# Attention, a rational MoE and a second MoE on one core: one scale chain for both halves of a weight chunk, five places for its float32 forms, and bounds spread by products with ones

## The chip, the cores and the metric

The kernel runs on one core of one Trainium2 chip. The metric is device time in microseconds (us), lower is better. Time before: 1236.59 us, the median of three runs (1235.79 to 1240.24).

## What is computed

```python
def _attn_ref(q, k, v, tau):                       # 4 batches, 8 heads, 576 rows, 64 wide
    scores = scale * np.matmul(q, k.transpose(0, 1, 3, 2))
    thresh = np.max(scores, axis=-1, keepdims=True) - tau
    scores = np.where(scores >= thresh, scores, -1000000000.0)
    ...
    return np.matmul(attn, v).astype(np.float32)

def _moe_ref(x, w_in, w_out, a, b):                # 2304 tokens, 512 -> 2048 -> 512
    h = x @ w_in
    ...
    g = P / (Q + 1e-06)                            # P cubic in h, Q quadratic in |h|
    return (g @ w_out).astype(np.float32)

def _moe2_ref(x, w_in, w_out):
    h = x @ w_in
    g = np.where(pos, h, np.where(neg, 0.0, (h + beta) ** 2 / (4.0 * beta)))
    return (g @ w_out).astype(np.float32)
```

The attention's output is the first expert's input, and the first expert's output the second's. The weights come as 64-bit floats.

## The kernel before

**Order of work.** For each of four batches b the first expert (m = 0) and then the second (m = 1) run over three token blocks j of 192 tokens and eight chunks i of 256 hidden columns: 192 steps in all, 24 to a phase. A step is `first_product` (24 matmuls of 192 columns, line L863, tile `ph`), a nonlinearity on ACT and DVE (`rational`, lines L744 to L757, for the first expert, `quadratic`, L808 to L810, for the second), a split of its result into two float16 parts (L209 on ACT, L213 on POOL, tile `gg`), and, three steps later, `second_product` (24 matmuls, L877, tile `acc`). The attention of batch 0 runs ahead of all steps in a transposed form (`first_attention`: `row_max` with DVE maxima L544, `transposed`, `sums`, `divide`). The attention of batches 1 to 3 runs beside the steps as 36 softmax rows of 128 queries each (`att_rows`: maximum L442, exponential L403, threshold L404, splits L412 to L415, a transposing DMA L417, products L430). A priority, `at(...)`, says where on the line of steps each piece belongs, and a scheduler writes the order of each engine's queue by these priorities and its own clock. Each engine runs its queue in that order.

**Weights.** Each chunk of an expert has two halves, x = 0 (`w_in`) and x = 1 (`w_out`), 16 halves per expert. A half is loaded (tile `rw`, 1 MB, L242), and three DVE instructions on 128x1024 words turn the 64-bit words into float32 (`as_float`, L229 to L231, tile `wt`). These float32 forms turn through N_WT = 3 places. Then comes the half's scale chain in `convert`:

- PE multiplies the bfloat16 tops by themselves (8 matmuls, L254, tile `pg`), and DVE takes the largest of each row (L255).
- `everywhere` spreads that bound over all partitions: a product of the bound, broadcast as the stationary operand, with the identity (L188, 128 columns of float32, two instructions) and a DVE maximum over the 128 columns (L189, tile `mw`).
- `root` makes a power of two and its inverse from it: three DVE instructions of one column, L169, L172 and L173 (tiles `f_w` and `pw`).
- `split` scales the float32 form in place on ACT (L218), copies it to float16 (L209) and lets POOL subtract in four pieces (L213). Only then is the place free.

The first expert's halves go into the resident chunks `wc` while `first_attention` runs, 16 halves over 45 steps of it (`make_half`), and a copy of each chunk goes to a scratch in memory. The second expert's halves (`stage_half`, tiles `wh`, two places of the same size as a `wt` place) follow and go to the scratch alone. `prep_pair` spreads the two bounds of q and k of a head pair in the same way (L188 twice, tile `pmmqke`; L189 on 256 columns, tile `mqke`), 16 times in the run.

Of the kernel before, what the change touches and what calls it, by code (L numbers as in the profile page):

```python
# [10 lines left out]
F32 = mybir.dt.float32  # L11
I32 = mybir.dt.int32
# [31 lines left out]
def tile_attention_moe_moe2(  # L44
# [148 lines left out]

    wide = w1_in.dtype != F32
# [7 lines left out]
    f_w = [[small(NCH, f"f_w{m}{x}", True) for x in range(2)] for m in range(2)]  # L202
    f_max = [[None, None], [None, None]]
    gram = small(NCH, "gram", True)
# [16 lines left out]
    def as_float(raw, name):  # L221
# [6 lines left out]
        t = mp.tile([P, E], I32, name="wt" + name, tag="wt", bufs=N_WT)  # L228
# [5 lines left out]
    def convert(m, i, x, dst, on_vector):  # L234

        if x == 0:
            raw = rp.tile([P, KT, CF * words], raw_type, name=f"rw{m}_{i}_0", tag="rw")
            src = w_in_dram[m][:, i * CF * words : (i + 1) * CF * words].rearrange("(kt p) f -> p kt f", p=P)
        else:
            raw = rp.tile([P, NF, DM * words], raw_type, name=f"rw{m}_{i}_1", tag="rw")  # L240
            src = w_out_dram[m][i * CF : (i + 1) * CF, :].rearrange("(f p) d -> p f d", p=P)
        (A if m == 0 and i == 0 else Q).dma_start(raw, src)  # L242
        name = f"{m}_{i}_{x}"
        src = as_float(raw.rearrange("p a b -> p (a b)"), name)
        hi, lo = dst[:, 0:E], dst[:, E : 2 * E]
        columns = m == 0 and x == 0
        bound = gram[:, i : i + 1] if columns else small(1, "mb" + name)
        pg = ps_1.tile([P, 512], F32, name="pg" + name, tag="aux")
        parts = NF if columns else 1
# [5 lines left out]
        V.tensor_reduce(bound, pg[:, 0 : parts * P], axis=AX.X, op=ALU.max)  # L255
        s = root("pw" + name, f_w[m][x][:, i : i + 1], everywhere("mw" + name, bound, 1), 2.0**64, even=m == 1 and x == 1)
        split(hi, lo, src, s, on_vector)
        if i == NCH - 1 and (m, x) != (0, 0):
            f_max[m][x] = small(1, f"f_max{m}{x}", True)
            V.tensor_reduce(f_max[m][x], f_w[m][x], axis=AX.X, op=ALU.max)  # L260
# [73 lines left out]
    def prep_pair(b, pr, on_vector=True):  # L334
# [12 lines left out]
        s = root(f"qkr{b}_{pr}", f, everywhere(f"mqke{b}_{pr}", mx, 2), 2.0**96, n=2)  # L347
# [342 lines left out]
    def moe1_consts(b):  # L690
# [6 lines left out]
        if b == 0:  # L697
# [3 lines left out]
            V.tensor_reduce(norm, gram, axis=AX.X, op=ALU.max)  # L701
# [187 lines left out]
    for n in range(N_FIRST):  # L889
        with at(36 * n / N_FIRST - 40):  # L890
            next(att)
        while halves and len(halves) * N_FIRST > 2 * NCH * (N_FIRST - 1 - n):
            with at(2.4 * (2 * NCH - len(halves)) - 39.5):
                i, x = halves.pop(0)
                make_half(0, i, x, chunks[0, i], False)
# [82 lines left out]
```

## Time and profile before

| | |
|---|---|
| median of three runs | 1236.59 us |
| profiled execution, its own time | 1239.17 us |
| its span, first to last instruction | 1237.1 us |
| busy in that span: PE, DVE, ACT, POOL | 1095.3, 979.3, 839.5, 542.7 us |
| mean granted clock of TensorE | 0.963 |

The profiled execution is 2.6 us above the median, and 2.1 us of its time lie outside the span. A busy share over the whole span mixes stretches with different limits. The rows further down are therefore taken by stretch: up to 230 us the first attention and the weights, then the 192 steps, the first 48 of them beside the attention of batch 1.

### The profile page before, as it was taken

To read this page: it belongs to the slowest core of one execution; us is meant where nothing else is said; L and a number is where in the kernel's file an instruction comes from. 1 tells how busy PE (TensorE), PEld (TensorE's weight loads), DVE (VectorE), ACT (ScalarE), POOL (GpSimd) and SP (SyncE) were. 2 spreads that over 40 slices of the span, in tenths; PEclk is the share of its full clock that TensorE was granted. 3 is DMA by queue.
4 is the path that set the end of the run, shared out by engine and by line. 5 is a ranking of instruction groups with operands and counts; after the bars stand their busy time and mean duration, and the time that the engine had idled before them with its cause. 6 is when DMAs were issued, how large, how long until landed. Compare 5 with 4: busy or idle time off the path is not lost.

```text
span 1237.1 us, 31750 instructions
## 1 busy us (share of the span) xinstructions
PE 1095.3 (89%) x12636; PEld 988.4 (80%) x12636; DVE 979.3 (79%) x2362; ACT 839.5 (68%) x1532; POOL 542.7 (44%) x698
## 2 busy tenths in 40 slices
PE   2778788588899999898888998998899999999998
PEld 1445456477888989898778888997888998999997
DVE  8887896999997377799997766899996768896431
ACT  2577777698887377677875766887675667775332
POOL 2445545656666266322564454223563553222221
PEclk9888888899899999999999999999999999999999
DMA  7677576635269158813785639422984467007000
GB/s 220 224 205 252 210 266 238 220 93 137 49 151 249 29 111 185 218 28 90 183 225 95 115 64 250 136 50 68 242 195 71 81 171 221 15 2 261 15 14 27
DMA packets 217845, 175.51 MB, mean 142 GB/s; under 512 B 179680, under 2 KB 190944, under 8 KB 209504
## 3 DMA queue, kind: packets, MB, share of 16 engines
q1 hardware_dynamic: 216464, 171.38, 52.6%
q8 instruction: 99, 1.62, 0.5%
q10 hardware_dynamic: 1232, 2.10, 0.5%
q14 instruction: 50, 0.41, 0.1%
HBM read 106.83 MB, written 21.50 MB: 104 GB/s over the span
## 4 chain that ended last, share of the span: by engine, by line
PE 40%; DVE 24%; DMA 11%; POOL 9%; issue 9%; ACT 6%; SPq 1%; DVEq 0%; ACTq 0%; POOLq 0%
PE acc L877 15%; PE ph L863 15%; DMA eT<-hl 8%; POOL hl L415 3%; PE pv L613 2%; PE pv L430 2%; DVE t L746 2%; POOL wh L213 2%; DVE e L404 2%; DVE t L751 2%; DVE sc L442 2%; POOL gg L213 1%; DVE t L757 1%; DVE t L748 1%; DVE t L747 1%
## 5 line engine op out<-in xcount | busy, mean ns | idle before, releaser
L877 PE MATMUL acc<-gg,wc 128*128 128x192 f16 x4608 | 427.6, 247 | 10.9 <-DVE mye L189 4.9
L863 PEld LDWEIGHTS <-wc 128*128 128x128 f16 x4608 | 388.9, 99 | 24.4 <-issue 16.5
L877 PEld LDWEIGHTS <-wc 128*128 128x128 f16 x4608 | 384.1, 98 | 12.6 <-issue 11.2
L213 POOL TENSOR_TENSOR gg<-t,gg 128x384 f16<-128x384 f32 x192 | 192.9, 1006 | 380.1 <-ACT gg L209 308.0
L863 PE MATMUL ph<-xT,wc 128*128 128x192 f16 x2304 | 218.1, 252 | 13.3 <-DVE t L748 13.2
L863 PE MATMUL ph<-yT,wc 128*128 128x192 f16 x2304 | 213.4, 246 | 3.7 <-DVE t L748 2.5
L415 POOL TENSOR_TENSOR hl<-e,hl 128x256 f16<-128x256 f32 x216 | 160.6, 764 | 0.0
L209 ACT CAST gg<-t 128x384 f16<-128x384 f32 x192 | 96.9, 508 | 75.1 <-DVE t L810 36.8
L809 DVE SCALAR_TENSOR_TENSOR t<-t,c 128x384 f32<-128x384 f32 x96 | 66.2, 690 | 88.9 <-ACT t L808 87.0
L404 DVE SCALAR_TENSOR_TENSOR e<-sc,nt,e 128x576 f32<-128x576 f32 x108 | 97.5, 903 | 28.1 <-ACT e L403 27.9
L413 POOL TENSOR_TENSOR hl<-e,hl 128x64 f16<-128x64 f32 x108 | 42.3, 391 | 147.7 <-ACT hl L412 134.0
L403 ACT ACTIVATE e<-sc,nt,con 128x576 f32<-128x576 f32 x108 | 93.3, 864 | 4.6 <-POOL hl L415 0.2
L808 ACT ACTIVATE t<-ph,c 128x384 f32<-128x384 f32 x96 | 63.9, 667 | 45.6 <-PE ph L863 45.3
L430 PE MATMUL pv<-v,eT 128*128 128x65 f16 (+3 forms) x1680 | 71.4, 195 | 25.2 <-DMA eT<-hl 24.1
L442 DVE TENSOR_SCALAR_CACHE_REDUCE sc<-s 128x576 f32<-128x576 f32 x108 | 80.8, 748 | 15.2 <-PE s L397 14.5
L412 ACT CAST hl<-e 128x576 f16<-128x576 f32 x108 | 72.1, 667 | 28.6 <-DVE e L404 28.0
L430 PEld LDWEIGHTS <-eT 128*128 128x128 f16 (+1 forms) x1680 | 64.0, 101 | 33.9 <-DMA eT<-hl 30.0
L744 ACT ACTIVATE t<-ph,sc 128x384 f32<-128x384 f32 x96 | 55.3, 576 | 50.6 <-PE ph L863 50.4
L213 POOL TENSOR_TENSOR wc<-wt,wc 128x256 f16<-128x256 f32 x64 | 55.1, 894 | 63.8 <-ACT wc L209 63.8
L749 ACT ACTIVATE t<-t,lc 128x384 f32<-128x384 f32 x96 | 67.8, 708 | 15.3 <-DVE t L746 14.9
L213 POOL TENSOR_TENSOR wh<-wt,wh 128x256 f16<-128x256 f32 x64 | 58.9, 950 | 35.8 <-ACT wh L209 35.7
L751 DVE SCALAR_TENSOR_TENSOR t<-t,ka,t 128x384 f32<-128x384 f32 x96 | 67.7, 705 | 8.7 <-ACT t L750 8.3
(238 smaller groups left out, 1910.9 us busy)
## 6 DMA issues: line engine op xcount, KB each, us to landing
wc<-scratch SPq DMA_DIRECT2D x56, 1024.0 KB, 5.9
rw<-in_moe_w_in_dram SPq DMA_DIRECT2D x15, 1024.0 KB, 5.7
rw<-in_moe_w_out_dram SPq DMA_DIRECT2D x15, 1024.0 KB, 5.4
scratch<-wc SPq DMA_DIRECT2D x8, 1024.0 KB, 4.5
scratch<-wh SPq DMA_DIRECT2D x16, 512.0 KB, 3.7
rqk<-in_q_dram SPq DMA_DIRECT2D x16, 256.0 KB, 3.1
rqk<-in_k_dram SPq DMA_DIRECT2D x16, 256.0 KB, 3.1
kT<-qkT SPq DMA_DIRECT2D x26, 144.0 KB, 2.5
```

Of the source, the lines that this page charges most:

```text
L209: A.copy(hi, src)
L213: G.tensor_tensor(lo[:, p], src[:, p], hi[:, p], op=ALU.subtract)
L403: A.activation(e, s, AF.Exp, bias=nb, scale=con[:, 0:1])
L404: V.scalar_tensor_tensor(e, s, th, e, op0=ALU.is_ge, op1=ALU.mult)
L412: A.copy(hi, e)
L415: G.tensor_tensor(lo_w[:, p], e[:, whole][:, p], hi[:, whole][:, p], op=ALU.subtract)
L430: T.matmul(pv[rows, 0:w], eT[:, c, cols], vv[:, h * NT + x if x < NT else H * NT + h, at : at + w], start=(n == 0), stop=(n == len(blocks) ...
L442: V.tensor_scalar(s, banks[:, 0:S], 1.0, -LARGEST, op0=ALU.mult, op1=ALU.max, accum_out=mx)
L749: A.activation(r, u, AF.Ln, bias=lc[:, 1:2], scale=lc[:, 0:1])
L751: V.scalar_tensor_tensor(s, s, ka[:, 0:1], r, op0=ALU.add, op1=ALU.mult)
L863: last = T.matmul(ph[:, f, :], w[:, wx, kt, f * P : (f + 1) * P], rhs, start=(n == 0), stop=(n == 3 * KT - 1))
L877: T.matmul(dst, w[:, wx, f, d * P : (d + 1) * P], gg[:, gx, f, :], start=(i == 0 and f == 0 and n == 0 and d % 2 == 0), stop=(i == NCH - 1 ...
```

## The change

- `make_half` handles the first expert's two halves of a chunk together. At x = 0 it loads, turns to float32 and takes the maxima (one per 128 columns, so two, into `gram`). At x = 1 it does the same with one maximum, then three products of one column with a constant tile of ones (L301, L302 of the changed file, six instructions where float32 takes two each) put the two bounds into two columns of PSUM, one `root` of two columns reads them there, and both halves are split. The column sums over the partitions take the place of the maxima, so no L189 follows.
- The float32 forms of the first expert turn through five places: the three of `wt` and the two of `wh`, which the second expert uses later.
- `total`, the product with ones, takes the place of `everywhere` in `prep_pair` and for the second expert's x = 1 halves.
- `gram` is 24 columns wide instead of 8, and its largest value is taken over the two columns that belong to `w_in`.

```diff
+    def total(name, src, n):
+
+        pm = ps_1.tile([P, 512], F32, name="ps" + name, tag="aux")[:, 0:n]
+        T.matmul(pm, one.to_broadcast([P, P]), src, start=True, stop=True)
+        return pm
...
-    def as_float(raw, name):
+    turn = [0]
+
+    def as_float(raw, name, first):
...
-        t = mp.tile([P, E], I32, name="wt" + name, tag="wt", bufs=N_WT)
+        n = turn[0] % (N_WT + N_WH)
+        turn[0] += 1
+        if first and n >= N_WT:
+            t = mp.tile([P, E], I32, name="wt" + name, tag="wh", bufs=N_WH)
+        else:
+            t = mp.tile([P, E], I32, name="wt" + name, tag="wt", bufs=N_WT)
...
-        s = root("pw" + name, f_w[m][x][:, i : i + 1], everywhere("mw" + name, bound, 1), 2.0**64, even=m == 1 and x == 1)
+        spread = (everywhere if x == 0 else total)("mw" + name, bound, 1)
+        s = root("pw" + name, f_w[m][x][:, i : i + 1], spread, 2.0**64, even=x == 1)
...
-    def make_half(m, i, x, wc, on_vector):
-        convert(m, i, x, wc[:, x * HALF : (x + 1) * HALF], on_vector)
-        if x == 1:
-            with at(8 + i):
-                Q.dma_start(scratch[m][i], wc)
+    first = {}
+
+    def make_half(i, x, wc):
+        first[x] = load_raw(0, i, x)
+        pg = ps_1.tile([P, 512], F32, name=f"pg0_{i}_{x}", tag="aux")
+        parts = 1 if x else NF
+        squares(pg, first[x], parts)
+        bound = gram[:, i]
+        V.tensor_reduce(bound[:, NF:] if x else bound[:, 0:NF], pg[:, 0 : parts * P].rearrange("p (n q) -> p n q", q=P),
+                        axis=AX.X, op=ALU.max)
+        if x == 0:
+            return
+        pm = ps_1.tile([P, 512], F32, name=f"psw0_{i}", tag="aux")[:, 0:2]
+        for c in range(NF):
+            T.matmul(pm[:, 0:1], one.to_broadcast([P, P]), bound[:, c : c + 1], start=c == 0, stop=c == NF - 1)
+        T.matmul(pm[:, 1:2], one.to_broadcast([P, P]), bound[:, NF:], start=True, stop=True)
+        s = root(f"pw0_{i}", f_w1[:, i], pm, 2.0**64, n=2)
+        for n in range(2):
+            split(wc[:, n * HALF : n * HALF + E], wc[:, n * HALF + E : (n + 1) * HALF], first[n], s[:, n : n + 1], False)
...
-        s = root(f"qkr{b}_{pr}", f, everywhere(f"mqke{b}_{pr}", mx, 2), 2.0**96, n=2)
+        s = root(f"qkr{b}_{pr}", f, total(f"mqke{b}_{pr}", mx, 2), 2.0**96, n=2)
```

The change also moves instructions, since the scheduler writes all queues anew. Line numbers of the changed kernel are higher: L169 and L172 keep their numbers, L188 stays, L229 to L231 become L246 to L248, L254 becomes L267, L255 becomes L280 and L295, L209 becomes L219, L218 becomes L228, L442 becomes L485, L544 becomes L587, L601 becomes L644, L746 to L757 become L789 to L800.

DVE's queue around the third chunk of the first expert, before. `wt_2_1` is the float32 form of chunk 2, half 1; `pw_2_0_s` and `pw_2_1_s` end the chains of its halves; `mx_1` are row maxima of the attention.

```order
L229 TENSOR_SCALAR wt_2_1_628<-rw_2_1_626 128x1024
L230 SCALAR_TENSOR_TENSOR wt_2_1_628<-rw_2_1_626,wt_2_1_628 128x1024
L544 TENSOR_REDUCE mx_1_554<-sm_00_555 128x1
L231 SCALAR_TENSOR_TENSOR wt_2_1_628<-rw_2_1_626,wt_2_1_628 128x1024
L255 TENSOR_REDUCE gram<-pg_2_0_513 128x1
L544 TENSOR_REDUCE mx_1_554<-sm_01_559 128x1
L189 TENSOR_REDUCE mw_2_0_523<-pmmw_2_0_524 128x1
L169 TENSOR_SCALAR f_w_135<-mw_2_0_523 128x1
L172 TENSOR_SCALAR f_w_135<-f_w_135 128x1
L173 RECIPROCAL pw_2_0_s<-f_w_135 128x1
L229 TENSOR_SCALAR wt_3_0_758<-rw_3_0_756 128x1024
L544 TENSOR_REDUCE mx_1_554<-sm_02_618 128x1
```

DVE's queue at the same place of the program, now. The chain of the whole chunk 2 ends with `pw_2_s`.

```order
L587 TENSOR_REDUCE mx_1_517<-sm_12_661 128x1
L172 TENSOR_SCALAR f_w_137<-f_w_137 128x2
L295 TENSOR_REDUCE gram<-pg_3_0_727 128x2
L173 RECIPROCAL pw_2_s<-f_w_137 128x2
L587 TENSOR_REDUCE mx_1_517<-sm_13_665 128x1
L587 TENSOR_REDUCE mx_1_517<-sm_t 128x4 x2
L587 TENSOR_REDUCE mx_1_517<-sm_r 128x1
L587 TENSOR_REDUCE mx_1_517<-sm_rt 128x1
L613 TENSOR_TENSOR mx_1_517<-mx_1_517 128x9
L616 TENSOR_SCALAR pcs_759<-mx_1_517 128x9
L618 SCALAR_TENSOR_TENSOR mx_1_517<-pcs_759,mx_1_517 128x9
L246 TENSOR_SCALAR wt_4_1_1086<-rw_4_1_1084 128x1024
```

Before, the chain of half 0 ends right behind the conversion of half 1, and the conversion of `wt_3_0` follows. Now the conversions of `wt_3_0`, `wt_3_1` and `wt_4_0` stand ahead of the chunk's one chain, and `wt_4_1`, which takes the place of `wt_2_0`, comes nine rows behind it.

ACT's queue for chunk 2, before: `low`, `et` belong to the attention.

```order
L218 ACTIVATE wt_2_0_509<-wt_2_0_509,pw_2_0_s 128x1024
L601 ACTIVATE low_0_4_718<-st_0_4_704,con_0_175 128x576
L209 CAST wc_2_148<-wt_2_0_509 128x1024
L601 ACTIVATE low_1_0_794<-st_1_0_786,con_0_175 128x576
L604 ACTIVATE et_0_4_717<-st_0_4_704,con_0_175 128x576
L604 ACTIVATE et_1_0_793<-st_1_0_786,con_0_175 128x576
```

ACT's queue for chunk 2, now: `x` and `d` are copies of the attention's sums.

```order
L228 ACTIVATE wt_2_0_486<-wt_2_0_486,pw_2_s 128x1024
L228 ACTIVATE wt_2_1_588<-wt_2_1_588,pw_2_s 128x1024
L664 COPY x_0_500<-pv_0_0_515 64x288
L663 COPY d_0_501<-pv_0_0_516 64x288
L664 COPY x_0_500<-pv_0_0_516 64x288
L644 ACTIVATE low_1_1_825<-st_1_1_817,con_0_173 128x576
L219 CAST wc_2_149<-wt_2_0_486 128x1024
L644 ACTIVATE low_1_2_842<-st_1_2_834,con_0_173 128x576
L219 CAST wc_2_149<-wt_2_1_588 128x1024
```

Half 0's copy to float16, on which POOL's subtraction waits, stood two rows behind its scaling; now the scaling of half 1 and four rows of the attention stand between.

DVE's queue in the first phase of steps, batch 0, from step 17 on (`t_0_2_1` is block 2, chunk 1 of the first expert), before. `sc`, `nt`, `e`, `xs`, `xT` belong to the attention rows of batch 1.

```order
L747 TENSOR_TENSOR t_0_2_1_3482<-t_0_2_1_3482,ph_0_2_1_3456 128x384
L444 TENSOR_SCALAR nt_1_0_0_5045<-mx_1_0_0_5044,con_1_3965 128x1
L465 TENSOR_TENSOR xs_0_2_4497<-pv_0_2_4444,rd_0_2_4494 128x128
L751 SCALAR_TENSOR_TENSOR t_0_2_0_3384<-t_0_2_0_3384,ka_1935,t_0_2_0_3383 128x384
L748 SCALAR_TENSOR_TENSOR t_0_2_1_3482<-t_0_2_1_3482,ka_1935,ph_0_2_1_3456 128x384
L476 TENSOR_TENSOR xT_1_3942<-xt_0_1_4417,xT_1_3942 128x64
L404 SCALAR_TENSOR_TENSOR e_0_2_2_4877<-sc_0_2_2_4873,nt_0_2_2_4872,e_0_2_2_4877 128x576
L757 SCALAR_TENSOR_TENSOR t_0_2_0_3383<-t_0_2_0_3383,t_0_2_0_3384 128x384
L442 TENSOR_SCALAR sc_1_0_1_5082,mx_1_0_1_5080<-s_1_0_1_5075 128x576
L746 SCALAR_TENSOR_TENSOR t_0_2_2_3581<-t_0_2_2_3581,qc 128x384
L747 TENSOR_TENSOR t_0_2_2_3582<-t_0_2_2_3582,ph_0_2_2_3556 128x384
L444 TENSOR_SCALAR nt_1_0_1_5081<-mx_1_0_1_5080,con_1_3965 128x1
```

DVE's queue from the same step on, now.

```order
L790 TENSOR_TENSOR t_0_2_1_3385<-t_0_2_1_3385,ph_0_2_1_3359 128x384
L800 SCALAR_TENSOR_TENSOR t_0_2_0_3288<-t_0_2_0_3288,t_0_2_0_3289 128x384
L791 SCALAR_TENSOR_TENSOR t_0_2_1_3385<-t_0_2_1_3385,ka_1852,ph_0_2_1_3359 128x384
L447 SCALAR_TENSOR_TENSOR e_0_2_1_4721<-sc_0_2_1_4717,nt_0_2_1_4716,e_0_2_1_4721 128x576
L794 SCALAR_TENSOR_TENSOR t_0_2_1_3385<-t_0_2_1_3385,ka_1852,t_0_2_1_3384 128x384
L789 SCALAR_TENSOR_TENSOR t_0_2_2_3484<-t_0_2_2_3484,qc 128x384
L800 SCALAR_TENSOR_TENSOR t_0_2_1_3384<-t_0_2_1_3384,t_0_2_1_3385 128x384
L790 TENSOR_TENSOR t_0_2_2_3485<-t_0_2_2_3485,ph_0_2_2_3459 128x384
L791 SCALAR_TENSOR_TENSOR t_0_2_2_3485<-t_0_2_2_3485,ka_1852,ph_0_2_2_3459 128x384
L794 SCALAR_TENSOR_TENSOR t_0_2_2_3485<-t_0_2_2_3485,ka_1852,t_0_2_2_3484 128x384
L789 SCALAR_TENSOR_TENSOR t_0_2_3_3631<-t_0_2_3_3631,qc 128x384
L790 TENSOR_TENSOR t_0_2_3_3632<-t_0_2_3_3632,ph_0_2_3_3606 128x384
```

Rows of the attention stood between the steps before; now the steps stand closer together. By the lists of the two queues 16 maxima L442 of batch 1 stand ahead of the first `quadratic` (step 24) before, and 9 now; ahead of step 29 they are 17 and 9, ahead of step 47 34 and 35, and from step 64 on the two lists differ by two rows at most.

## Rows read from the trace of the kernel before

**Rows 1.** Stretches: length, busy us (instructions) of PE, PEld, DVE, ACT, POOL; clock, DMA

```profile
0.00:45.00 45.00, 18.99 (x121) 11.52 (x121) 39.30 (x102) 15.55 (x25) 10.31 (x25) 1.00 0.63 197
45.00:230.00 185.00, 147.49 (x897) 95.75 (x898) 150.75 (x321) 136.77 (x214) 98.64 (x110) 0.84 0.71 238
230.00:370.00 140.00, 116.37 (x1321) 107.34 (x1319) 136.11 (x321) 119.60 (x222) 92.44 (x103) 0.93 0.47 120
...
435.00:503.00 68.00, 63.61 (x843) 57.67 (x841) 51.04 (x137) 48.73 (x94) 41.40 (x62) 0.97 0.76 161
503.00:1020.00 517.00, 477.45 (x6110) 448.71 (x6108) 432.23 (x1100) 369.50 (x703) 222.51 (x307) 0.99 0.58 132
```

**Rows 2.** Chain that ended last, 38 to 60 us: start, us, what

```profile
43.42 1.15 ACT wt L218
...
45.58 7.49 POOL wc L213 x8
...
53.10 1.16 DVE wt L229
```

**Rows 3.** The same chain, 45 to 230 us, its shares by line

```profile
by line: PE pv L613 15.3%; POOL wc L213 7.5%; POOL wh L213 6.2%; DVE wt L230 5.7%; DVE wt L231 5.0%; DVE wt L229 5.0%; issue 4.7%; ACT wt L218 4.2%; DMA rw<-in_moe_w_in_dram 3.5%; PE st L598 3.2%; PE st L596 3.2%; DVE mx L544 3.2%; PE st L5
```

**Rows 4.** Groups of instructions, DVE, 0 to 291 us: count, busy us, mean ns

```profile
L189 DVE TENSOR_REDUCE mw<-pmmw 128x1 f32<-128x128 f32 x32 | 9.1, 283 | 6.0 <-PE pmmw L188 6.0
...
L169 DVE TENSOR_SCALAR f_w<-mw 128x1 int32<-128x1 int32 x32 | 4.7, 145 | 0.3
...
L172 DVE TENSOR_SCALAR f_w<-f_w 128x1 f32<-128x1 f32 x32 | 4.7, 148 | 0.4
...
L173 DVE RECIPROCAL pw_s<-f_w 128x1 f32<-128x1 f32 x32 | 5.0, 156 | 0.5
...
L189 DVE TENSOR_REDUCE mqke<-pmmqke 128x2 f32<-128x256 f32 x6 | 2.5, 414 | 0.0
L169 DVE TENSOR_SCALAR qkf<-mqke 128x2 int32<-128x2 int32 x6 | 2.4, 408 | 0.0
...
L172 DVE TENSOR_SCALAR qkf<-qkf 128x2 f32<-128x2 f32 x6 | 1.8, 300 | 0.0
```

**Rows 5.** Waits of DVE, 0 to 291 us: total us, times, longest us

```profile
DVE mw L189 <- PE pmmw L188: 6.0, 6, 2.2
DVE wt L229 <- POOL wh L213: 5.7, 6, 1.8
...
DVE wt L229 <- POOL wc L213: 4.1, 5, 1.8
```

**Rows 6.** Line L188 on PE, whole run: ns min/median/max

```profile
L188 PEld LDWEIGHTS pmmqke<-ident,mqk x64: 185/190/338, 7.8 to 937.3; 128*128 128x128 f32 x64
L188 PE MATMUL pmmqke<-ident,mqk x64: 271/275/582, 7.8 to 937.4; 128*128 128x128 f32 x64
```

**Rows 7.** Groups of instructions, ACT, 0 to 186 us

```profile
L218 ACT ACTIVATE wt<-wt,pw_s 128x1024 f32<-128x1024 f32 x21 | 24.1, 1146 | 9.9 <-DVE pw_s L173 7.5 <-DVE f_max L260 2.2
...
L209 ACT CAST wc<-wt 128x1024 f16<-128x1024 f32 x16 | 16.6, 1040 | 0.1
```

**Rows 8.** The page's costliest groups

```profile
L404 DVE SCALAR_TENSOR_TENSOR e<-sc,nt,e 128x576 f32<-128x576 f32 x108 | 97.5, 903 | 28.1 <-ACT e L403 27.9
...
L213 POOL TENSOR_TENSOR wc<-wt,wc 128x256 f16<-128x256 f32 x64 | 55.1, 894 | 63.8 <-ACT wc L209 63.8
```

**Rows 9.** Groups of instructions, 435 to 503 us

```profile
L877 PE MATMUL acc<-gg,wc 128*128 128x192 f16 x271 | 27.1, 250 | 0.0
...
L442 DVE TENSOR_SCALAR_CACHE_REDUCE sc<-s 128x576 f32<-128x576 f32 x18 | 13.5, 748 | 2.4 <-PE s L397 2.4
```

**Rows 10.** Chain that ended last, 400 to 412 us

```profile
403.72 1.98 PE ph L863 x24
```

**Rows 11.** Lines L230 and L213: ns min/median/max

```profile
L230 DVE SCALAR_TENSOR_TENSOR wt<-rw,wt x23: 1206/1225/1710, 10.7 to 183.2; 128x1024 int32<-128x1024 int32 x23
...
L213 POOL TENSOR_TENSOR wc<-wt,wc x64: 662/672/1650, 26.7 to 154.3; 128x256 f16<-128x256 f32 x64
```

More of the change, by code (lines that the diff above doesn't have):

```diff
@@ L190, in everywhere @@
         return r
+    one = small(1, "one", True)
+    G.memset(one, 1.0)
+    def total(name, src, n):
+        pm = ps_1.tile([P, 512], F32, name="ps" + name, tag="aux")[:, 0:n]
+        T.matmul(pm, one.to_broadcast([P, P]), src, start=True, stop=True)
+        return pm
     wide = w1_in.dtype != F32
@@ L200, in tile_attention_moe_moe2 @@
     scratch = [dp.tile([NCH, P, 2 * HALF], F16, name=f"scratch{m}") for m in range(2)]
-    f_w = [[small(NCH, f"f_w{m}{x}", True) for x in range(2)] for m in range(2)]
+    f_w1 = cp.tile([P, NCH, 2], F32, name="f_w0")
+    f_w = [[f_w1[:, :, x] for x in range(2)], [small(NCH, f"f_w1{x}", True) for x in range(2)]]
     f_max = [[None, None], [None, None]]
-    gram = small(NCH, "gram", True)
+    gram = cp.tile([P, NCH, NF + 1], F32, name="gram")
     def split(hi, lo, src, scale=None, on_vector=True):
@@ L232, in as_float, with load_raw, squares @@
         return t.bitcast(F32)
-    def convert(m, i, x, dst, on_vector):
+    def load_raw(m, i, x):
+        name = f"{m}_{i}_{x}"
         if x == 0:
-            raw = rp.tile([P, KT, CF * words], raw_type, name=f"rw{m}_{i}_0", tag="rw")
+            raw = rp.tile([P, KT, CF * words], raw_type, name=f"rw{name}", tag="rw")
             src = w_in_dram[m][:, i * CF * words : (i + 1) * CF * words].rearrange("(kt p) f -> p kt f", p=P)
         else:
-            raw = rp.tile([P, NF, DM * words], raw_type, name=f"rw{m}_{i}_1", tag="rw")
+            raw = rp.tile([P, NF, DM * words], raw_type, name=f"rw{name}", tag="rw")
             src = w_out_dram[m][i * CF : (i + 1) * CF, :].rearrange("(f p) d -> p f d", p=P)
         (A if m == 0 and i == 0 else Q).dma_start(raw, src)
[L243 to L249, printed above, removed]
+        return as_float(raw.rearrange("p a b -> p (a b)"), name, m == 0)
+    def squares(pg, src, parts):
         top = src.bitcast(BF16).rearrange("p (n c f w) -> p n c f w", c=parts, f=P, w=2)[..., 1]
@@ new lines, in tile_attention_moe_moe2 @@
+    first = {}
[16 more added lines that the diff above has]
+            split(wc[:, n * HALF : n * HALF + E], wc[:, n * HALF + E : (n + 1) * HALF], first[n], s[:, n : n + 1], False)
+        if i == NCH - 1:
+            largest(0, 1)
+        with at(8 + i):
+            Q.dma_start(scratch[0][i], wc)
@@ L700, in moe1_consts @@
             A.activation(gram, gram, AF.Exp, scale=0.5)
[L701 removed]
+            V.tensor_reduce(norm, gram[:, :, 0:NF], axis=AX.XY, op=ALU.max)
             norms.append(everywhere("nrm", norm, 1, True))
@@ L894, in tile_attention_moe_moe2 @@
                 i, x = halves.pop(0)
-                make_half(0, i, x, chunks[0, i], False)
+                make_half(i, x, chunks[0, i])
     beside = [[] for _ in steps]
```

18 lines of the change are left out of this document (13 added, 5 removed).

## Prediction

> **What bounds the kernel now.** I read the stretches first, then the chain that ended last, then groups and waits. The stretches [rows 1] show no single limit. Up to 45 us DVE is busy 39.3 of 45 us and PE is not half busy: the kernel starts at DVE's pace. From 45 to 230 us DVE has 150.8 and PE 147.5 of 185 us, at a TensorE clock of 0.84, a mean between its two levels, 1.2 and 2.4 GHz. From 230 to 370 us DVE is the limit, 136.1 of 140 us. Later PE leads: 63.6 of 68 us from 435 to 503 us, 477.5 of 517 us from 503 to 1020 us.
>
> The chain shows how a weight chunk holds things up. ACT scales a half, POOL subtracts for 7.49 us in eight pieces, and only then does DVE start the next conversion [rows 2]: it stood at a place that POOL had not freed. DVE waited so for 4.1 us on the first expert's halves and 5.7 us on the second's, and 6.0 us for the product of `everywhere` [rows 5]. Yet between 45 and 230 us the chain runs over PE at least as much as over DVE: `pv` on PE has 15.3%, the three conversions and the row maxima on DVE 18.9% together [rows 3].
>
> **The sum.** It is made against the profiled execution's own time, 1239.2 us, which lies 2.6 us above the median of 1236.6.
>
> *Scale chains on DVE.* A half's chain now costs a maximum of 0.283 us and three one-column rows of 0.145, 0.148 and 0.156 us [rows 4], 0.732 us, so 1.46 us a chunk. The change drops both maxima and keeps three rows of two columns. No row shows one that reads two columns from PSUM. The nearest are the two-column rows of a head pair, 0.408 and 0.300 us [rows 4]; with the same inverse that makes 0.86 us. At the one-column price it would be 0.45 us. So a chunk saves 0.60 to 1.01 us. I take 0.60, the like form: 8 chunks, 4.8 us, with 8.1 us as the far end. The maximum over the squares keeps its columns and its price.
>
> *Head pairs and the second expert.* Each of 16 pairs loses a maximum of 0.414 us [rows 4], six of them before 291 us: 2.5 us. The second expert's eight x = 1 halves lose 0.283 us each: 2.3 us. DVE thus loses 9.6 us of work before 291 us: 2.0 up to 45 us (two chunks, two pairs), 6.4 from there to 230 us (six chunks, two pairs, seven halves), 1.1 after it.
>
> *What of it lies on the path.* All of the first 2.0 and the last 1.1 us, where DVE is near full [rows 1]. Of the 6.4 us between, no more than DVE's busy share, 0.81, or 5.2 us, and no less than its share of the chain, 0.19, or 1.2 us. I take half, 3.2 us. Together **6.3 us**.
>
> *Waits.* The 6.0 us for the spreading product were waited at 32 places; 24 are left (eight pairs of halves and the second expert's 16), so a quarter goes: **1.5 us**. For the wait on places I take nothing. Five places could end the first expert's 4.1 us, but a half now keeps its place until its chunk's chain is through; this is the first rival below.
>
> *PE.* An `everywhere` of one column is two instructions of 0.275 us, with a weight load of 0.190 us each [rows 6]. A chunk now has four of these and will have six with a single column, priced between their loads alone (1.14 us) and today's rows (1.65 us), against 1.10 us: 0 to 4.4 us dearer over eight chunks. A head pair goes from four to two: from 1.10 us to 0.38 to 0.55 us, so 0.55 to 0.72 us less. The four pairs before 230 us give back 2.2 to 2.9 us, and I set that stretch to zero. Of the other twelve pairs, 7.6 us of PE work, eight lie in the stretch from 503 us on, where PE is 92% busy, and four beside batch 1. I count somewhat under half, **3 us**; the ends are 0 and 7.6.
>
> *The order of the steps.* By the queue lists, eight attention rows of batch 1 that now stand ahead of step 29 move behind it. Each costs DVE 0.748 [rows 9] and 0.903 us [rows 8], so 13.2 us leave a stretch that DVE fills. They come back where PE leads. There PE was busy 63.6 us for 18 rows [rows 9] and 271/24, or 11.3, steps of 2 x 1.98 us [rows 10]: 63.6 - 44.7 = 18.9 us, 1.05 us a row, 8.4 us for eight. The net is -4.8 us; I take **4 us**, as a mixed stretch never reaches its floor. The ends are -13 us, if PE's idle time swallows the rows, and +4 us, if the steps alone run no faster. From step 64 on the lists agree within two rows, so nothing more is moved.
>
> The rest is free: the wider `gram` and the constant are a few rows once, beside work of other engines. DMA bytes do not change, and loads of the first expert move by a slot or two on SP.
>
> Sum: 6.3 + 1.5 + 3 + 4 = 14.8, so 1239.2 - 15 = 1224 us for such an execution, or **1222 us** for a median. That is -1.2%. About 0.5%, 6 us, is what a measurement of this kernel can tell from no change: 1230.4 and 1242.8 us are the bounds.
>
> **Rivals.**
>
> *Slower, by pairs that hold their places.* A place is free after scaling, copy and four pieces of subtraction: 1.146 + 1.040 [rows 7] + 4 x 0.894 us [rows 8] = 5.8 us behind the end of the chain. Now both halves wait for one chain, and the second is free another 5.8 us later. `wt_4_1` stands nine rows behind the chain whose half it must follow, and on ACT the scaling of the other half and four attention rows now stand ahead of the copy. If chunks 2 to 7 each cost DVE one wait of 5.8 us, 34.6 us replace the 9.8 us of today, and all row maxima queued behind wait too: 1236.6 - 15 + 25 = 1246 us. It decides from 4.1 us a chunk on, (14.8 + 9.8)/6. For it: the chain of waits already runs through POOL's pieces [rows 2, 3]. Against it: five places hold two and a half chunks, and in most chunks twenty and more DVE rows lie between. Chance 0.17.
>
> *No change, because PE and the attention set the first 230 us.* Then DVE's 6.4 us turn into idle time there, and the moved rows cost what they gave. What stays is 2 us at the start and 1 us of the late pairs: 1233.6 us. For it: PE's lines lead the chain [rows 3] and the clock there is low. Chance 0.18.
>
> *DVE and POOL in each other's way.* The conversion L230 takes 1.206 us at least and 1.710 at most, a POOL piece 0.662 and 1.650 [rows 11]. POOL's pieces will come eight in a row, under conversions that no longer stop for them. Half of them now run at 1.225 us or less, the median. If each of the first expert's 32 two-input conversions (L230 and L231) took the longest time, they would cost up to 32 x 0.485 = 15.5 us more; half of it on the path makes -7 us of -15: 1229 us. The Trainium skill, page "SBUF — State Buffer", section "Who interferes with whom", states that a VectorE instruction with two SBUF inputs and a GpSimd instruction that reads SBUF exclude each other for the whole instruction. By that rule, both spreads of durations agree with the trace, and a denser POOL would meet more conversions. Chance 0.12.
>
> *More.* The 4.1 us of waits end and PE's idle time takes in half of the moved rows: -23 us, 1213 us. Chance 0.08.
>
> That the change does not do what it says can be left out: the lists show one chain a chunk and 63 DVE rows fewer.
>
> **Numbers.** My forecast has 0.45. Faster by over 0.5%: 0.45 + 0.12 + 0.08 = 0.65; within it 0.18; slower 0.17. The range runs from 1210 us, the DVE savings at their far ends with the rows hidden, to 1242 us, which leaves out most of the slower case and little else.
>
> **What would show it.** Right: L189 on `mqke` and 24 on `mw` gone; DVE's busy time before the steps some 8 us less; the first `ph` of the steps, and with it the end of the stretch now at 370 us, earlier by about 10 us; 18 rows or more beside steps 31 to 47. Wrong: DVE waits on POOL in L246 above 20 us in all (the slower rival); L247 and L248 at means above 1.5 us (the ports); a first stage as long as now with DVE idle longer (PE).

## The result and the profile after

The changed kernel took 1252.6 us, the median of four runs (1249.5 to 1258.5), beside 1238.4 us for the kernel before on the same chip. The ratio is 1.0122, with a 95% interval from 1.0087 to 1.0156: **slower by 1.2%**, where the prediction had 1.2% faster. The profiled execution took 1258.5 us, 6 us above that median, with a span of 1256.6 us.

The stretches of the changed kernel, to be held against [rows 1] (busy us of each engine and instructions in brackets, then the granted clock as a share of 2.4 GHz, the DMA share and GB/s):

```profile
core 0: us, PE busy (x) PEld busy (x) DVE busy (x) ACT busy (x) POOL busy (x), PEclk, DMA share, GB/s
0.00:45.00 45.00, 18.08 (x97) 10.74 (x98) 38.49 (x84) 11.44 (x21) 7.77 (x22) 1.00 0.71 215
45.00:230.00 185.00, 150.97 (x894) 96.69 (x891) 135.49 (x268) 131.72 (x204) 95.72 (x106) 0.87 0.66 212
230.00:370.00 140.00, 108.62 (x1138) 99.46 (x1139) 132.20 (x288) 112.51 (x209) 89.24 (x95) 0.88 0.44 118
...
503.00:1020.00 517.00, 476.21 (x6109) 444.97 (x6107) 426.52 (x1100) 371.47 (x706) 224.07 (x308) 0.99 0.57 135
```

From 45 to 230 us DVE was busy 135.5 us in the place of 150.8, and its idle time rose from 34.2 to 49.5 us: nothing was done sooner for it. The stretch from 503 us on holds nearly the same work as before, only later.

Where the loss is made shows in the first product of step 48, the first step of batch 1: PE's line turns from the tile `yT` to `xT` there. The timeline of that line on PE (count, duration in ns, first and last start in us), before:

```profile
L863 PE MATMUL ph<-xT,wc x9: 246/246/246, 495.0 to 495.8; 128*128 128x192 f16 x9
```

and after:

```profile
L906 PE MATMUL ph<-xT,wc x9: 246/246/246, 519.6 to 522.9; 128*128 128x192 f16 x9
```

Step 48 starts 24.6 us later, and the last second product ends 19.6 us later (1249.9 against 1230.3 us). All of the loss of the changed kernel lies ahead of step 48. Two stretches split that time, up to the first second product and from there to step 48; before:

```profile
0.00:244.00 244.00, 175.77 (x1110) 115.71 (x1111) 203.97 (x448) 163.41 (x255) 117.94 (x144) 0.87 0.68 227
244.00:495.00 251.00, 227.45 (x2811) 212.95 (x2809) 208.25 (x525) 187.69 (x360) 147.73 (x184) 0.97 0.54 129
```

and after:

```profile
0.00:261.90 261.90, 188.31 (x1119) 123.47 (x1120) 204.41 (x400) 163.21 (x257) 125.04 (x148) 0.87 0.67 217
261.90:519.60 257.70, 228.17 (x2826) 212.36 (x2824) 209.71 (x522) 189.66 (x362) 141.31 (x183) 0.96 0.50 122
```

DVE's busy time up to step 48 is 412.2 us before and 414.1 after, its idle time 82.8 and 105.5. So 22.7 of the 24.6 us are idle time of DVE, 17.5 of them ahead of the first second product.

The scale chains did what they were to do. Groups of instructions on DVE up to 291 us (busy us, mean ns, idle time before them):

```profile
L172 DVE TENSOR_SCALAR f_w<-f_w 128x2 f32<-128x2 f32 x8 | 2.8, 344 | 0.1
...
L189 DVE TENSOR_REDUCE mw<-pmmw 128x1 f32<-128x128 f32 x8 | 2.2, 279 | 4.3 <-PE pmmw L188 4.3
...
L173 DVE RECIPROCAL pw_s<-f_w 128x2 f32<-128x2 f32 x8 | 1.3, 162 | 0.1
...
L169 DVE TENSOR_SCALAR f_w<-psw 128x2 int32<-128x2 int32 x8 | 1.2, 155 | 1.8 <-PE psw L302 1.7
```

A chunk's chain takes 0.155 + 0.344 + 0.162 = 0.66 us of DVE, where two maxima and six rows took 1.46 us [rows 4]; 24 of the 32 maxima `mw` are gone. DVE's waits up to 291 us (us in total, times, longest), to be held against [rows 5]:

```profile
DVE mx L587 <- PE sm L584: 10.3, 6, 4.1
DVE wt L246 <- DMA rw<-in_moe_w_in_dram: 9.9, 5, 3.2
DVE gram L295 <- PE pg L267: 8.1, 7, 4.7
DVE wt L246 <- POOL wh L223: 6.8, 7, 1.8
DVE mw L189 <- PE pmmw L188: 4.3, 1, 4.3
...
DVE f_w L169 <- PE psw L302: 1.7, 3, 0.8
...
DVE f_w L169 <- PE psmw L200: 1.4, 1, 1.4
```

No conversion waits for POOL's `wc` any more (4.1 us before). In its place stand waits of another kind: for the attention's products `sm` 10.3 us (5.6 before), for loads 9.9 us (3.7). ACT shows a wait at the start too, in its timeline of the first two chunks (start, us, instruction, idle time before it and who ended it):

```profile
37.17 1.23 ACT L219 CAST qk<-rqk 128x576 f16<-128x576 f32 x2
44.30 2.19 ACT L228 ACTIVATE wt<-wt,pw_s 128x1024 f32<-128x1024 f32 x2 [5.90 <-DVE pw_s L173]
46.39 1.98 ACT L219 CAST wc<-wt 128x1024 f16<-128x1024 f32 x2
48.49 2.19 ACT L228 ACTIVATE wt<-wt,pw_s 128x1024 f32<-128x1024 f32 x2
52.61 1.37 ACT L644 ACTIVATE low<-st,con 128x576 bf16<-128x576 f32 x2 [1.94 <-PE st L641]
```

ACT idles 5.9 us for the chunk's chain, scales two halves at a time, and comes to the attention's first `low` at 52.6 us (47.2 before). The first pair's divide starts at 101 us (86 before). That alone is not the cause: it starts at 103 us in E11 below, which loses nothing that a measurement shows.

### The profile page after: what moved, and what is told of

Its sections match the earlier page's. It is cut to its first block, busy times and chain, and to the rows that moved or that the text cites. A ratio compares the mean times of both kernels' runs of the same rounds, so it can differ in the third digit from the quotient of the medians.

```text
span 1256.6 us, 31657 instructions
## 1 busy us (share of the span) xinstructions
PE 1104.9 (88%) x12620; PEld 990.4 (79%) x12620; DVE 972.1 (77%) x2298; ACT 840.9 (67%) x1532; POOL 543.1 (43%) x699
## 4 chain that ended last, share of the span: by engine, by line
PE 33%; DVE 17%; DMA 10%; ACT 8%; issue 6%; POOL 5%; SPq 1%; ACTq 0%; DVEq 0%; POOLq 0%
PE acc L920 15%; PE ph L906 14%; DMA eT<-hl 6%; POOL hl L458 3%; DVE e L447 3%; DMA rqk<-in_q_dram 2%; DVE t L794 2%; DMA qkT<-qk 2%; PE pv L473 2%; DVE sc L485 1%; DVE t L800 1%; ACT hl L455 1%; DVE t L791 1%; DVE t L789 1%; DVE t L790 1%
## 5 line engine op out<-in xcount | busy, mean ns | idle before, releaser
L906 PE MATMUL ph<-yT,wc 128*128 128x192 f16 x2304 | 216.8, 247 | 2.5 <-DVE t L853 1.1
L219 ACT CAST gg<-t 128x384 f16<-128x384 f32 x192 | 97.2, 508 | 73.3 <-DVE t L853 41.1
L485 DVE TENSOR_SCALAR_CACHE_REDUCE sc<-s 128x576 f32<-128x576 f32 x108 | 80.8, 749 | 12.3 <-PE s L440 11.8
L439 PE MATMUL s<-qkT 128*128 128x512 f16 (+1 forms) x240 | 63.5, 293 | 18.8 <-DVE sc L485 17.1
L794 DVE SCALAR_TENSOR_TENSOR t<-t,ka,t 128x384 f32<-128x384 f32 x96 | 70.8, 737 | 11.9 <-ACT t L793 11.5
## 6 DMA issues: line engine op xcount, KB each, us to landing
scratch<-wh SPq DMA_DIRECT2D x16, 512.0 KB, 3.3
```

Source lines behind the costliest of these rows:

```text
L219: A.copy(hi, src)
L485: V.tensor_scalar(s, banks[:, 0:S], 1.0, -LARGEST, op0=ALU.mult, op1=ALU.max, accum_out=mx)
L794: V.scalar_tensor_tensor(s, s, ka[:, 0:1], r, op0=ALU.add, op1=ALU.mult)
L906: last = T.matmul(ph[:, f, :], w[:, wx, kt, f * P : (f + 1) * P], rhs, start=(n == 0), stop=(n == 3 * KT - 1))
```

## The experiments

The change has three parts: **A**, products with ones for head pairs and the second expert; **B**, the shared chain of the first expert (products with ones in it); **C**, five places. Ratios are against the kernel before on the same chip; the start of step 48 is that of the profiled execution.

| kernel | median us | ratio, 95% interval | step 48 starts, us |
|---|---|---|---|
| before | 1236 to 1238 | 1 | 495.0 |
| the change (A, B, C) | 1252.6 | 1.0122 [1.0087, 1.0156] | 519.6 |
| E1: A | 1236.1 | 0.9991 [0.9969, 1.0013] | 498.4 |
| E2: C | 1252.7 | 1.0124 [1.0085, 1.0162] | 515.3 |
| E3: A, B | 1260.2 | 1.0180 [1.0140, 1.0221] | 523.2 |
| E4: B, C | 1263.9 | 1.0215 [1.0178, 1.0251] | 511.6 |
| E5: the change, rows earlier | 1257.8 | 1.0182 [1.0136, 1.0228] | 517.0 |
| E6: before, rows later | 1235.1 | 0.9979 [0.9952, 1.0006] | 496.7 |
| E7: the change, halves later | 1259.1 | 1.0189 [1.0153, 1.0225] | 520.6 |
| E8: before, rows earlier | 1241.8 | 1.0031 [1.0009, 1.0053] | 497.9 |
| E9: C, held | 1250.7 | 1.0125 [1.0095, 1.0154] | 515.3 |
| E10: the change, held | 1243.4 | 1.0069 [1.0041, 1.0097] | 505.6 |
| E11: A, C | 1237.4 | 1.0017 [0.9993, 1.0041] | 503.0 |
| E12: B | 1258.0 | 1.0191 [1.0150, 1.0233] | 511.5 |
| E13: A, C, first half late | 1240.6 | 1.0018 [0.9993, 1.0042] | 507.6 |
| E14: before, first half late | 1259.9 | 1.0187 [1.0158, 1.0215] | 519.5 |
| E15: A, C, own chains with ones | 1250.3 | 1.0106 [1.0076, 1.0136] | 512.0 |
| E16: A, own chains with ones | 1242.4 | 1.0048 [1.0026, 1.0071] | 503.9 |
| E17: A, C, shared chain with maxima | 1242.6 | 1.0053 [1.0033, 1.0072] | 508.4 |
| E18: A, C, held | 1244.7 | 1.0077 [1.0049, 1.0105] | 507.9 |

The last column separates two groups. The six kernels up to 1.0031 start step 48 at 495 to 508 us, the ten from 1.0106 on at 511 to 523 us. It does not rank the kernels inside a group: from the start of step 48 to the end of the last second product they need 723 to 743 us, and E4, the slowest, starts step 48 at 511.6 us and loses some 8 us behind it. Up to step 48 no engine of the kernel before is busy throughout: DVE was busy 412 and PE 403 of those 495 us, though DVE fills the part from 230 to 370 us [rows 1].

### The three parts, alone and together

E1 puts `total` into the kernel before, for pairs and the second expert alone:

```diff
-    s = root(..., everywhere("mw" + name, bound, 1), ...)
+    s = root(..., (total if m and x else everywhere)("mw" + name, bound, 1), ...)
...
-    s = root(f"qkr{b}_{pr}", f, everywhere(f"mqke{b}_{pr}", mx, 2), 2.0**96, n=2)
+    s = root(f"qkr{b}_{pr}", f, total(f"mqke{b}_{pr}", mx, 2), 2.0**96, n=2)
```

> The kernel before with one part of the change: head pairs and the second expert's x = 1 halves spread their bound by a product with ones (no maximum behind it); every half of the first expert keeps its own chain, three places. Theory A (five places: conversions go ahead of the first attention in the queues, and the attention is late) and theory B (the shared chain: scalings and copies of two halves come in a burst on ACT, ahead of the attention's rows) both expect no loss here: 16 x 0.41 + 8 x 0.28 us of DVE work less, some 2 to 5 us of it on the path, so 1233 to 1238 us, with the first second-product matmul of the steps at 240 to 245 us as before (244.0). Theory C (any re-made order of the queues costs the first attention its place) expects a loss here too: that matmul at 250 us or later, 1245 us or more.

It measured 0.9991, a gain of 1 us (by the interval, from a gain of 3.8 to a loss of 1.6 us). The first second-product matmul came at 257 us and not at 240 to 245, which was theory C's sign, yet nothing was lost by it. E2 puts the five places of the diff into the kernel before.

> The kernel before with one part of the change: the float32 forms turn through five places; own chains, spreading by maxima. Theory A: the conversions run ahead of the first attention, the loads become their limit, and pair 0's divide starts at 95 us or later (86 before, 101 in the changed kernel); 1245 to 1253 us. Theory B: no loss, 1234 to 1240 us, divide of pair 0 at 84 to 90 us, since the scalings still come one by one. Theory C: a loss as with every new order.

1.0124, which is theory A's time, but without its sign: pair 0's divide starts at 90 us, as theory B had it. Pair 3's starts at 257 us (224 before). E3 takes the five places out of the changed kernel:

```diff
-        if first and n >= N_WT:
+        if False:
```

> The changed kernel with three places in the place of five: shared chain and products with ones stay. Theory A: the loss is gone, 1225 to 1240 us, pair 0's divide at 90 us or earlier. Theory B: the loss stays or grows, since a pair now holds two of three places through the chain: 1250 us or more, with DVE's waits on POOL in the conversions above 20 us in all. Theory C: a loss.

1.0180: worse, so theory A's cure is none. Theory B has the time and not the sign: the attention is on time (pair 0's divide at 89 us), and the conversions wait only 2.9 us on `wc` and 5.5 on `wh`, where over 20 us were expected. E4 puts the maxima back outside the shared chain (`total` becomes `everywhere` in both places).

> The changed kernel with the maxima back in the head pairs and in the second expert's halves (the products with ones stay in the first expert's shared chain alone), five places. Theories A and B: still slower than before, 1248 to 1260 us, with pair 0's divide near 100 us, since both their causes are still in it. If it is near 1238 us, the loss came from the new order that the products with ones of pairs and second expert brought (theory C, or these products themselves).

1.0215, above the range of both theories. E11 (E1 and E2 together) and E12 (the changed kernel with both edits of E3 and E4) complete the eight combinations.

> The kernel before with products with ones in head pairs and the second expert, and five places, but own chains. Its conversions 4 to 6 stand behind 5, 10 and 15 row maxima of the attention (12, 13, 15 before; 5, 10, 13 with five places alone). Theory O: between, 1240 to 1252 us. Theory S with five places at fault: 1248 to 1254 us. If only the shared chain cost anything: 1234 to 1238 us.

> The kernel before with the shared chain alone: three places, maxima for head pairs and for the second expert. Conversions 3, 5 and 7 stand behind 12, 19 and 24 row maxima (3, 13, 17 before), and the last ones of the second expert beside step 18. Both theories: slower, 1252 to 1264 us, since a pair holds two of three places; the first attention is not late (pair 3's divide at 215 to 228 us), the second expert's conversions are (last one ends after 300 us, 251 before), and step 48 starts at 510 us or later.

1.0017 and 1.0191. In every background the shared chain makes the kernel slower: by 1.9% with three places (E12, and E3 against E1), by 0.9 and 1.05% with five (E4 against E2, the change against E11). A and C together cost nothing that a measurement shows. But the parts do not add up. C costs 1.2% alone (E2) and 0.3% beside A (E11 against E1), and in the full change it takes back 0.6% (against E3); A brings 0.9 to 1.1% with five places and 0.1% with three. Why C costs so much alone stays open. E12's conversions were late as expected: the last one ends at 323 us (251 before).

### Rows of batch 1: a theory that fell

After the first four, fewer attention rows ahead of step 24 went with a longer time. E5, E6 and E8 alter that order alone, E7 the place of the conversions alone:

```diff
-ATTENTION = {1: (18, 50), 2: (60, 100), 3: (108, 147)}
+ATTENTION = {1: (15, 47), 2: (60, 100), 3: (108, 147)}
```

for E5 in the changed kernel; (22, 50) for E6 and (14, 50) for E8 in the kernel before; for E7, `- 38` in the place of `- 39.5` in the due time of the halves.

> The changed kernel with one pair of numbers altered: the units of batch 1's attention are due over steps 15 to 47 in the place of 18 to 50. The order of the first attention and of the conversions stays what it is in the changed kernel; 20 rows of batch 1's attention stand ahead of step 24 in DVE's queue (16 in the kernel before, 9 in the changed one). Theory R (rows: what is lost is paid where rows stand beside the second expert's first 24 steps; every configuration run so far is the slower, the fewer rows stand ahead of step 24: 20 and 16 rows 1236 and 1238 us, 13 and 9 rows 1253, 5 and 6 rows 1260 and 1264): 1236 to 1243 us, and the start of step 48 back at 500 to 505 us. Theory F (first stage: the first 262 us are 18 us too long, and this is not made good): 1249 to 1254 us. The first matmul of the second product stays near 262 us by both.

> The kernel before with one pair of numbers altered: batch 1's attention due over steps 22 to 50 in the place of 18 to 50; no instruction is added or removed, and the first 230 us keep their order. 12 rows stand ahead of step 24, 12 ahead of step 32 (16 and 18 in the kernel before). Theory R: slower, 1244 to 1256 us, and step 48 starts at 502 us or later. Theory F: no change, 1234 to 1241 us. By the prediction's term on moved rows it would be 2 to 3 us faster.

> The changed kernel with the conversions of the first expert due 1.5 steps later: the eleventh conversion then stands behind 26 of the first attention's row maxima as in the kernel before (34 in the changed kernel), and 12 rows of batch 1 ahead of step 24. Theory F, in the form that the place of the conversions among the first attention's rows is at fault: the first second-product matmul comes at 250 us or earlier (262), and the time falls to 1235 to 1243 us. Theory R: 12 rows, so little better than the changed kernel, 1246 to 1254 us.

> The kernel before with batch 1's attention due over steps 14 to 50: 21 rows stand ahead of step 24, 22 ahead of step 32. Theory R, if it holds beyond the kernel's own setting: 1228 to 1238 us. Theory F: no change. If rows ahead of step 24 are dearer than beside the second expert, as the prediction's term had it: 1240 to 1246 us.

1.0182, 0.9979, 1.0189 and 1.0031. Theory R falls: with 20 rows ahead of step 24 the changed kernel is no faster, and with 12 the kernel before is no slower. Theory F is the nearer in E5 (1257.8 us, above its range) and has E6 right; E8, at 1241.8 us, is as the prediction's term had it. As a rule theory F does not hold either: the first second-product matmul comes at 257 us in E1 and at 267 us in E13, which lose nothing, and at 230 to 232 us in E12 and E14, which lose 1.9%. The length of the first stage by itself does not tell the time. Between E8 and E6, 21 against 12 rows, the kernel before differs by 0.0052 of 1238, 6.4 us or 0.7 us a row, and rows are the dearer ahead of step 24, as the prediction had it. E7 says that the due time of the halves is no cure: the twelfth to the sixteenth conversion moved back behind 24 to 34 of the row maxima (31 to 36 in the changed kernel, 25 to 36 before), and it got worse than either theory had it.

### Holding the old order

E9, E10 and E18 tie each conversion on DVE and each scaling on ACT, in the order of issue alone, behind as many rows of the first attention as in the kernel before:

```diff
+        with tc.issue_after(maxima[behind - 1]) if behind else nullcontext():
             V.tensor_scalar(t, src[:, :, 1], 0x07FFFFFF, 3, ...)
...
+            with tc.issue_after(exps[behind - 1]) if behind else nullcontext():
                 A.activation(src, src, AF.Copy, scale=scale)
```

> The kernel before with five places (the run of places alone took 1252.7 us), and each conversion and each scaling now held, in the order of issue alone, behind as many of the first attention's row maxima on DVE and of its `low` and `et` on ACT as in the kernel before; the places stay five and no work is added. Theory O (order: three places throttled the conversions; with five they are ready early, are queued ahead of the attention's rows on the in-order engines, and the attention is late): the loss goes, 1235 to 1243 us, pair 3's divide at 218 to 232 us (224 before, 257 with five places alone), and the first second-product matmul at 240 to 256 us. Theory S (the five places themselves, through the loads and through the places they share with the second expert's halves): 1248 to 1256 us, as without the hold.

> The changed kernel with the same hold. Theory O: pair 0's divide at 90 us or earlier (101 in the changed kernel, 86 before), the first second-product matmul at 250 us or earlier, and 1228 to 1243 us. Theory S, in the form that the shared chain costs by itself (the first half's scaling waits for the second half's conversion, so ACT and POOL idle and then get two halves at once): 1248 us or more, with the conversions in their old places in the queue.

> Products with ones in pairs and second expert, five places and own chains (1.0017 of before as the scheduler orders it), with each conversion and scaling held in the order of issue behind as many of the first attention's rows as in the kernel before. No work differs. Theory N: the order does not matter by more than 0.3%, 0.999 to 1.005. Theory R2 (at five places the order alone is worth about 1%): 1.006 or more, and then the 1% of the products with ones cannot be told from it.

1.0125, 1.0069 and 1.0077. E9 is as theory S had it, E18 as theory R2; E10 lies at the edge of theory O's time without its signs. The attention was still late in E9 (first second-product matmul at 258 us) and E10 (255 us, pair 0's divide at 108 us). The hold does nothing for C alone, takes back nearly half of the changed kernel's loss, and costs A and C together 0.6%. So theory O does not hold as a rule, but the order alone, with not one instruction more or less, moves a kernel with five places by up to 0.7% either way: the changed kernel's instructions ran at 1.0069, 1.0122, 1.0182 and 1.0189 in four orders.

### Lateness, or the new form

E13 (on E11) and E14 (on the kernel before) share nothing. They only hold the first half's spreading maximum and three scale rows behind the second half's maximum over its squares:

```diff
+        if m == 0 and x == 0:
+            late[i] = finish
+            return
+        if m == 0:
+            with tc.issue_after(red.ins):
+                late.pop(i)()
+        finish()
```

> The run with products with ones in pairs and second expert and five places (1.0017 of before), own chains of three one-column rows as before, but the first half's spreading maximum and rows now issue on DVE behind the second half's maximum over its squares. Nothing is shared. Theory L (lateness is what costs): 1.007 to 1.015 of before, 1245 to 1255 us, as when the chain is shared (1.0122). Theory N (the new form of the chain costs): 1.000 to 1.004.

> The same delay put into the kernel before: three places, maxima everywhere, own chains, the first half's rows behind the second half's maximum. Theory L: 1.014 to 1.025 of before, as the shared chain with three places (1.0191), 1254 to 1267 us, with the second expert's last conversion after 300 us. Theory N: under 1.005.

E14 measured 1.0187, as much as the shared chain with three places (1.0191). So **at three places the lateness alone costs as much as the whole shared chain**: a half that must wait for its neighbour's conversion holds its place longer. DVE's waits up to 291 us in E14:

```profile
DVE mx L556 <- PE sm L553: 14.6, 15, 2.6
DVE wt L229 <- POOL wc L213: 12.4, 6, 4.8
```

The wait on `wc` tripled (4.1 us before). In E12 it was 3.3 us, so there the delay stands in the order of the queue and not in a wait. What E3, E12 and E14 share is late conversions: the sixteenth stands behind 47 or 48 of the first attention's 48 row maxima (36 before), and the last one starts at 318 to 326 us (250 before, 237 to 273 in E1, E6, E8 and E16, which also have three places). What it costs appears later. In E14 eight conversions are still to do after 230 us, here the timeline of their first line:

```profile
L229 DVE TENSOR_SCALAR wt<-rw x8: 682/1424/1484, 232.1 to 314.7; 128x1024 int32<-128x1024 int32 x8
```

The kernel before has three:

```profile
L229 DVE TENSOR_SCALAR wt<-rw x3: 680/694/1481, 229.6 to 245.0; 128x1024 int32<-128x1024 int32 x3
```

They take DVE's time where DVE is full, and attention rows give way. The maxima of batch 1's rows by stretch in E14 (two records a row):

```profile
230.00:370.00 140.00, 3.00 (x8) 0.88 0.50 161
370.00:520.00 150.00, 23.42 (x62) 0.95 0.69 144
```

and in the kernel before:

```profile
230.00:370.00 140.00, 10.54 (x28) 0.93 0.47 120
370.00:495.00 125.00, 15.09 (x40) 1.00 0.62 145
```

31 rows in the place of 20 stand beside the second expert's 24 steps, and those take 155 us (364.6 to 519.5) in the place of 125. With five places the same lateness costs nothing (E13, 1.0018 beside 1.0017 for E11, as theory N had it). E13 has part A and E14 has not, but A is worth only 0.1% at three places. E13's waits:

```profile
DVE mb L273 <- PE pg L272: 8.6, 6, 3.9
DVE wt L245 <- DMA rw<-in_moe_w_in_dram: 5.9, 4, 2.3
DVE mx L573 <- PE sm L570: 5.3, 5, 2.6
DVE wt L245 <- POOL wh L222: 4.8, 7, 1.3
...
DVE wt L245 <- POOL wc L222: 1.2, 2, 0.7
```

Of the wait on `wc` 1.2 us are left. E15 and E16 have the other half: own chains as soon as the squares are there, but bounds of the first expert spread by products with ones. E17 has the shared chain, with the bounds spread by maxima.

```diff
-        if x == 0:
-            return
...
+        s = root(f"pw0_{i}_{x}", f_w1[:, i, x : x + 1], pm, 2.0**64)
```

```diff
-        for c in range(NF):
-            T.matmul(pm[:, 0:1], one.to_broadcast([P, P]), bound[:, c : c + 1], start=c == 0, stop=c == NF - 1)
-        T.matmul(pm[:, 1:2], one.to_broadcast([P, P]), bound[:, NF:], start=True, stop=True)
+        pm = everywhere(f"mw0_{i}", bound, 2)
```

> The changed kernel with each half of the first expert on its own chain again, as soon as its own squares are there; bounds spread by products with ones everywhere but in the second expert's x = 0 halves, five places. Theory L: the loss is gone, 0.993 to 1.003 of before, 1228 to 1241 us. Theory N: still 1.007 or more.

> The same with three places: 16 maxima of 0.283 us fewer on DVE than in the run with products with ones in pairs and second expert alone (0.9991). Theory L: 0.992 to 1.000 of before, 1226 to 1238 us. Theory N: 1.007 or more.

> The changed kernel with the shared chain and five places, but the chunk's two bounds are spread by the two-column maximum of the kernel before (two products with the identity, one maximum over 256 columns) in the place of products with ones. If the products with ones in the first expert's chain are what costs at five places (theory N): 1.000 to 1.004 of before, 1236 to 1242 us. If sharing costs there too: 1.009 to 1.015. If it is neither, but the order that the scheduler happens to make (theory R2): anywhere from 1.002 to 1.020.

1.0106, 1.0048 and 1.0053: E15 is as theory N had it, E16 between the two, and E17, by its median, fits theory R2 alone. Kernels with products with ones in the first expert are 0.7 to 0.9% above those with maxima at five places (the change against E17, E15 against E11) and 0.6% at three (E16 against E1), though DVE does less in them. Of the same size is what a new order alone did (E18 against E11, E10, E7), and E17 lies above E13 as well. So at five places the change's 1.2% is made up of about 0.2% for A and C (E11), 0.2 to 0.4% for the sharing (the change against E15, E17 against E11) and 0.7 to 0.9% for the products with ones in the first expert's chain. **It stays open** whether the products themselves or the order that the scheduler made around them cost this; no run keeps the order and changes the products.

None of the 18 beats the kernel before by what a measurement can tell; E6, at 0.9979, comes nearest.

## Why the prediction was wrong

- **The work on DVE** was sized well where the edit is: a chunk's chain saves 1.46 - 0.66 = 0.80 us, between the stated 0.60 and 1.01. Over the span DVE's busy time fell from 979.3 to 972.1 us. Up to step 48 it did not fall (412.2 and 414.1 us), as other rows took longer there, the conversions by 3.9 us, and one attention row more lay ahead of it.
- **What of it lies on the path** is the step that failed: "Together **6.3 us**". None of it showed. From 45 to 230 us DVE did 15.3 us less and idled 15.3 us more. Of the work, the maxima L189 are 6.2 us; another 7.9 us are conversions, 22 in this stretch in the place of 25, of which five in the place of three were left over after 230 us. The prediction took DVE's share of the time, or of the chain, for a share of the path. E1 tests part of it by itself: 16 maxima of 0.41 us and eight of 0.28 us go, and the time hardly moves.
- **For the wait on places I take nothing.** The wait did end, and that too brought nothing (E11). The rival "pairs hold their places" named a mechanism that exists: with three places it costs 1.9%, 23 us (E14). It was priced at 25 us for five places, so the nearness is luck. With five places the waits on POOL's `wc` are gone from the changed kernel, and those in L246 come to 6.8 us on `wh` where its sign was 20, so the change as made did not lose by it.
- **A term was missing**: every queue was written anew, and the sum looked only at the rows of batch 1; what the new order does to the waits stood at nothing. DVE's idle time up to step 48 rose by 22.7 us, which is nearly all of the loss there. The lists already showed the new order, the scalings of both halves side by side and the first attention's row maxima in other places. Orders of the same instructions differ by up to 1.2% here (E10 to E7). The order of the kernel before may be one of the better ones, as 16 of the 18 kernels lie above 1; most of them change more than the order, so this is not shown.
- **Waits for the spreading product**: 6.0 us fell to 4.3, about the 1.5 us predicted, but the rows behind products with ones now wait 1.7 and 1.4 us (`psw`, `psmw`). Together that is 7.4 us, so nothing was gained.
- **PE, 3 us for late pairs, and the pairs' and second expert's 4.8 us of DVE**: together 1 us of gain (E1, interval -3.8 to +1.6 us).
- **Rows, 4 us**: right in sign and near in size, 0.7 us a row between E6 and E8, so 5 to 6 us for eight. They could not show beside the loss.
- **DVE and POOL in each other's way**: the 64 two-input conversions went from 42.5 + 44.1 to 44.5 + 45.2 us, 3.1 us over both experts, where the rival's far end was 15.5 us for the first alone, and the means of L247 and L248, 1.39 and 1.41 us, stay under its sign of 1.5. The loss is far larger.
- **No change, because PE and the attention set the first 230 us** came closest in its reason: the saved work did turn into idle time of DVE. Of its sign, the first stage was longer than before and not equal (the first `ph` starts at 193 us in the place of 186). It took the order for granted as well.

## What to carry to other kernels

In a stretch where the engines wait for each other, work taken off the busiest one can turn into idle time, as it did here; measure one part alone, and one reordering without any change of work, before pricing a saving there. A chain shared by two tiles makes the first as late as the second and holds its buffer that long: count the buffers first, since the same lateness cost 1.9% with three and nothing with five. Where a scheduler writes the queues, compare the lists of every engine in the stretch that sets the time, not only where the edit is.

## What the runs showed of the hardware

A conversion's time goes with what POOL does beside it. Of the 32 first lines (L229) in the kernel before, the 24 with POOL busy for under a tenth of their time took 0.69 us in the mean, none over 0.70; the seven with POOL busy for nine tenths or more took 0.85 to 1.48 us, 1.15 in the mean. For L230 the means were 1.22 (19) and 1.56 us (8). In E14 they were 0.69 (15) and 1.21 us (14), and 1.22 (15) and 1.60 us (11). The prediction had named the two-input lines; the first, with one input, suffers too, and more for its length. The Trainium skill, page "SBUF — State Buffer", section "Who interferes with whom", states that `tensor_scalar` can hold the port pair that DVE and GpSimd share when it runs in a two-port mode; the durations agree with that.

A float32 product with a single column is hardly shorter than one with 128. Groups on PE up to 291 us in the changed kernel (mean ns behind the busy time):

```profile
L301 PE MATMUL psw<-gram,one 128*128 128x1 f32 x32 | 6.1, 293 | 3.2 <-DVE gram L295 3.2
...
L200 PE MATMUL psmw<-mb,one 128*128 128x1 f32 x16 | 3.3, 275 | 5.8 <-DVE mb L280 5.8
```

These means mix both levels of the clock, and the profile models the ends of products. At a granted clock of 1.0 the median of L301 was 250 ns, against 275 for the identity's 128 columns (L188, `pmmw`, before); at 0.5 they were 352 and 422 ns. So a chunk's six instructions take more of PE than the four they replace; what its products with ones save is the maximum on DVE alone. There, a row of two columns that reads PSUM cost hardly more than one of one column (L169, 0.155 us against 0.145 before); of the eight rows L172 behind it three took 0.63 to 0.68 us and the others 0.15 to 0.17.
